# Talking-heads attention and an MLP on one core: x loaded a unit ahead, stores two units behind, first keys from two queues, and the second mixing with 128-column weights on two row halves

## The chip, the core and the metric

One core of a Trainium2 chip runs the whole program. The metric is device time in microseconds (us), the median of the runs of one kernel. Engines are named as in the profile: PE is TensorE (PEld its weight loads, which overlap its matmuls), DVE VectorE, ACT ScalarE, POOL GpSimd, SP SyncE. SP, ACT and POOL also issue DMAs from their own queues, in the order of their programs.

## What is computed

```python
def attn(q, k, v, w_pre, w_post):                 # 4 batches, 12 heads, 448 rows, 64 wide
    scores = (1 / 8) * q @ k.transpose(0, 1, 3, 2)
    scores = einsum('bhij,hg->bgij', scores, w_pre)      # first mixing of the heads
    attn = softmax(scores)                               # over j
    attn = einsum('bhij,hg->bgij', attn, w_post)         # second mixing
    return attn @ v

x = attn(...).transpose(0, 2, 1, 3).reshape(1792, 768)
h = x @ w_in                                      # 768 x 2048
out = maximum(0.01 * h, h) @ w_out                # 2048 x 768
```

All inputs and the output are float32.

## The kernel before, in words

The work has two stages. The **attention stage** goes over 16 chunks: each of the four batches has its 448 query rows cut into chunks of 120, 120, 120 and 88 rows. A chunk takes three **units** (`s` = 0, 1, 2), and `at` = 3n + s counts the 48 units. Several chunks are in flight: unit (n, s) does

- `scores` for chunk n + 2, two head pairs: PE writes `pss`, ACT moves it to the tile `st` (line 198);
- `first` for the next unit's rows: the first mixing, PE, `psm`, from the tiles `r`; then `maxima` (DVE, line 231) and `power` (ACT, line 241, the exponentials `et`);
- `weights` for this unit: DVE makes `kp`, the second mixing's matrix divided by the row sums;
- `mix` in two parts (lines 259 to 298): the second mixing, PE, `psa`. The weights of these matmuls are columns of `et`, which is why `mix` also transposes; the moving side is `kp`. Part 0 takes key chunks 0 and 1 and ACT copies its result to `at` (line 308); part 1 takes key chunks 2 and 3 and DVE copies it. Key chunk 3 holds 64 keys. A matmul of `mix` works on 64 of the 128 rows (`b`) and 64 of the 128 output partitions (`z`), so four of them lie side by side in the array;
- `values` for chunk n - 1: PE, `psx` from `at` and `vt`, then from `half` and `vend`; DVE copies it to `xo` (line 333) and SP stores a chunk's `xo` to `x_dram` (line 340).

Between chunks the scores change their layout by DMA: `regroup` (line 207) reads `st` and writes the twelve tiles `r`, even ones from SP's queue, odd ones from POOL's (line 212). The table `REGROUP` says in which of the chunk's twelve slots (three units of four) the pairs of tiles are issued.

Beside this, the MLP's weights arrive in a packed form and are put together in the attention stage by `Narrow`: SP loads `craw` (line 96), ACT spreads it (lines 102 and 103), DVE assembles (108 to 115), POOL joins (119 and 120) and SP stores `w` to `w_dram` (line 123). A store is issued at the start of the unit after the join.

The last six units (`at` = 42 to 47) run through `end_period` (line 625). In them `x_work` brings in the attention's result for the **MLP stage**: `load_x` (line 357) issues four DMAs `xr<-x_dram` (line 362), and `prep_x` (line 366) makes seven operands of them, one for each `k`. An operand is a pair `xh` (ACT, line 386) and `xl` (DVE, line 387); for k = 2, 3, 4 and 6 POOL first takes a difference (lines 374, 377, 379, 381). `x_plan` says in which slot which load or operand is made. The tiles `xr` come from a pool of five; the difference of k = 2 has a tile of its own, `xt`.

The MLP stage (`hidden`, `project`) multiplies in three products of split operands and is one long run of matmuls on PE.

Before the first unit come the warm-up matmuls `idle`, the first queries and the first keys: SP issues twelve DMAs `kt<-in_k` in a row (line 156), then the queries of chunk 1 (line 167).

Every engine works through its instructions in the order in which this code issues them (`pin`); only the plain calls of the MLP stage are left to the scheduler.

Of the kernel before, what the change touches and what calls it, by code (L numbers as in the profile page):

```python
# [8 lines left out]
F32 = mybir.dt.float32  # L9
# [14 lines left out]
PIECE = 384  # L24
RUN = 2
QUAD = 2 * ROWS
REGROUP = (0, 1, 3, 5, 7, 9)


def chunks_of(S):  # L30
# [4 lines left out]
def kernel(  # L35
# [10 lines left out]
    nc = tc.nc  # L46
    B, P, NJ, H, D = v.shape
    S = k.shape[3]
# [7 lines left out]
    HALF = SLOTS // 2  # L56
    HP = P // 2
    HC = NC // 2
    XS = 8
    HALF_IN = HC * P  # L60
    scale = 1.0 / math.sqrt(D)
    assert NC == 2 * HC and NF % 2 == 0 and B % 2 == 0
# [65 lines left out]
    pool = pools(left, "left")  # L128
# [5 lines left out]
    pool = pools(psum, "left")  # L134
# [3 lines left out]
    pool = pools(right, "right")  # L138
    p_q = pool("q", 2)
    p_k = pool("k", 2 * NPAIR)  # L140
    pool = pools(top, "left")
# [3 lines left out]
    pin = tc.keep_in_program_order  # L145
# [3 lines left out]

    k_t, q_t, v_t, s_t, r_t, e_t, kp_t, at_t, xo_t = ({} for _ in range(9))  # L150

    def load_k(b, a):
        t = k_t[b, a] = p_k.tile([P, S], F32, tag="k", name="kt")
        for e in range(2):
            up = slice(D * e, D * (e + 1))
            pin(nc.sync.dma_start(t[up], k[b, up, 2 * a + e, :]))

    def width(n):
        return -(-chunks[n][2] // QUAD) * QUAD
# [99 lines left out]
    def mix(n, s, part):  # L259

        sg = chunks[n][3][s]
        if s == part == 0:
            at_t[n] = (
                p_at.tile([P, (NJ - 1) * H, CHUNK], F32, tag="at", name="at"),
                p_at.tile([P, NPAIR, CHUNK], F32, tag="half", name="half"),
            )  # L270
        at, half = at_t[n]
        es, kp, nu, R = e_t[n, s][0], kp_t[n, s], len(sg), ROWS // 2
        ps = ps_x.tile([P, 2, 512], F32, tag="x", name="psa")
        per = nu * ROWS
        outs, done = [], 0
        for c in ((0, 1), (2, NJ - 1))[part]:
            nh = H if c < NJ - 1 else NPAIR
            outs.append(ps[:, :, done:done + nh * per])
            out = outs[-1].rearrange("p b (h u w) -> p b h u w", h=nh, w=ROWS)
            done += nh * per  # L280
            for g, e in enumerate(es):
                for z in range(2):
                    for b in range(2):
                        up, to = slice(HP * b, HP * (b + 1)), slice(HP * z, HP * (z + 1))
                        keys, step = (c * P + HP * z, 1) if nh == H else (c * P, 2)
                        mm(
                            out[to, b, :, g // 2, R * (g % 2):R * (g % 2 + 1)], e[up, keys:keys + HP],
                            kp[up, g, (z if step == 2 else 0)::step], start=True, stop=True,
                        )
        cols = slice(QUAD * sg[0], QUAD * sg[0] + QUAD * nu)  # L290
        if part == 0:
            moves = [(at[:, :2 * H], ps[:, :, :done], nc.scalar.copy)]
        else:
            moves = [(at[:, 2 * H:], outs[0], nc.vector.tensor_copy), (half, outs[1], nc.vector.tensor_copy)]
        return [(
            copy, to[:, :, cols].rearrange("p h (u b w) -> p b h u w", b=2, w=ROWS),
            src.rearrange("p b (h u w) -> p b h u w", u=nu, w=ROWS),
        ) for to, src, copy in moves]
# [44 lines left out]
    pl = {}  # L343

    def open_x():
        pool = pools(mlp, "right")
        pl.update(xr=pool("xr", 5), xs=[pool("xs0", XS)])

    def open_mlp():
        pool = pools(mlp, "right")  # L350
# [13 lines left out]
    X_PARTS = 7  # L364

    def prep_x(p, c, k, add=nc.vector, hold=free):

        x = [[xr_t[p, c, h, e] for e in range(2)] for h in range(2)]
        if k == 2:
            xr_t[p, c] = pl["xr"].tile([P, S], F32, tag="xr", name="xt")
            hold(add.tensor_sub(xr_t[p, c], x[0][1], x[0][0]))
        t = xr_t.get((p, c))
        if k == 3:
            hold(add.tensor_sub(x[0][1], x[1][1], x[0][1]))
        if k == 4:
            hold(add.tensor_sub(t, x[1][1], t))
        if k == 6:  # L380
            hold(add.tensor_sub(x[1][0], x[1][0], t))
        name, raw = ((1, x[0][0]), (2, x[1][0]), (5, t), (7, x[0][1]), (6, t), (3, x[1][1]), (4, x[1][0]))[k]
        pool = pl["xs"][X_PARTS * c + k >= XS]
        hi = pool.tile([P, S], F32R, tag="xh", name="xh")
        lo = pool.tile([P, S], F32R, tag="xl", name="xl")
        hold(nc.scalar.copy(hi, raw))
        hold(nc.vector.tensor_sub(lo, raw, hi.bitcast(F32)))
        x_t[name, c] = hi, lo
# [132 lines left out]
    nc.scalar.activation(warm, warm, AF.Exp)  # L521
    load_q(0, nc.scalar, nc.sync)
    for a in range(NPAIR):
        load_k(0, a)
    load_q(1)
    for t in r_all:
        nc.vector.memset(t[:LOW], 0.0)
# [62 lines left out]
            piece.assemble()  # L590
            joining.append(piece)

    x_plan = {0: [-1], 9: [6, -2], 17: [13, -3]}
    x_plan.update({i + 3: [i] for i in range(6)})
    x_plan.update({i + 4: [i] for i in range(7, 13)})
    x_plan.update({i + 5: [i] for i in range(14, 19)})

    def x_work(n, t):
        for i in x_plan.get(t + SLOTS * (n - NCK + 2), ()):
# [25 lines left out]
    def end_period(n, s):  # L625

        nonlocal kept, pending
        at = 3 * n + s - 42
        if kept:
            keep_x(*kept)  # L630
            kept = None
        for piece in joining:
            piece.join()
        storing.extend(joining)
        joining.clear()
        if at == 0:
            right.close()
            open_x()
            store_x(n - 2)
        if at == 3:  # L640
            top.close()
            open_mlp()
            load_wi(0)
            store_x(n - 2)
        if at == 4:
            mixed.close()
            pool = pools(mlp, "right")
            pl.update(ws=pool("ws", 1), ps_h=pool("ps_h", 1, space=PSUM))
        early, late = ((2, 0), (2, 1), (2, 1), (1, 0), (0, 0), (0, 0))[at]
        if pending:  # L650
            keep_at(mix(*pending, 1))
            pending = None
        weights(n, s)
        dues = [first(*left_quads.pop(0)) for _ in range(early)]
        for due in dues:
            maxima(*due)
        for c in range(NJ):
            transfers(n, s, c)
            x_work(n, NJ * s + c)
        for due in dues:  # L660
            power(*due)
        keep_at(mix(n, s, 0))
        assemble()
        keep_x(*values(n - 1, s))
        keep_at(mix(n, s, 1))
        for _ in range(late):
            due = first(*left_quads.pop(0))
            maxima(*due)
            power(*due)
        if at == 4:  # L670
            prep_wi(0, 0, pin)
        if at == 5:
            prep_wi(0, 1, pin)

    pending = None
    for n in range(NCK):
        b = chunks[n][0]
        last = n == NCK - 1
        for s in range(3):
# [2 lines left out]
            nxt = (n, s + 1) if s < 2 else (n + 1, 0)  # L682
            to, pair = n + 2, 2 * s

            for piece in storing:
                piece.store()
            storing.clear()
            if at >= 42:
                end_period(n, s)
                continue  # L690
# [12 lines left out]
            weights(n, s)  # L703
            for piece in joining:
                piece.join()
            storing.extend(joining)
            joining.clear()
            if pending:
                keep_at(mix(*pending, 1))
# [25 lines left out]
    hidden(0, 0, 0)  # L735
    for s in range(3):
        keep_x(*values(NCK - 1, s))
        if s:
            prep_x(0, HC - 1, X_PARTS - 3 + s, nc.gpsimd, pin)
    store_x(NCK - 1)  # L740
    psum.close()
    left.close()
# [108 lines left out]
```

## Time and profile before

| | us |
|---|---|
| median of 3 runs | 905.76 (905.28 to 906.59) |
| profiled execution, its time | 906.61 |
| profiled execution, its span | 904.7 |
| PE busy | 815.0, 90% of the span |
| DVE, ACT, POOL busy | 591.4, 487.7, 170.9 |

The span runs from the program's first instruction to its last. Busy time is a mean over stages: the attention stage ends near 443 us, and what bounds it is not what bounds the MLP stage. The granted clock of PE stands beside each stretch in the table by stretch. A matmul's end is modelled, so the pace of a row of matmuls is read from their starts, or from the time that the whole row takes.

### The profile page before, as it was taken

The page shows a single profiled execution, that of the slowest core. Times are in us where ns is not written, and L with a number is a line of the kernel's source. Part 1 is how long each engine was busy: PE and PEld are TensorE (multiplying, and loading weights), DVE is VectorE, ACT ScalarE, POOL GpSimd, SP SyncE. Part 2 cuts the span into 40 slices and gives each one's busy share as a digit, 9 for nine tenths or more (in the row PEclk, how much of TensorE's full clock was granted, in tenths as well). Part 3 has the DMA queues.
Part 4 walks back from the last instruction along what each step waited for, and adds up shares of the span by engine and source line. Part 5 has one row for each costly group of instructions (what it writes and reads, how often), then busy time and mean ns, then how long its engine had stood idle before and what let it go on. Part 6 is the DMA issues. An engine that isn't in the chain of part 4 may idle for free.

```text
span 904.7 us, 25819 instructions
## 1 busy us (share of the span) xinstructions
PE 815.0 (90%) x10904; PEld 652.1 (72%) x10904; DVE 591.4 (65%) x1063; ACT 487.7 (54%) x952; POOL 170.9 (19%) x224
## 2 busy tenths in 40 slices
PE   7789887989987989846779999999999999999998
PEld 2356655656655656634669999998999999999997
DVE  5478674786865767636588777876956656663433
ACT  3578784876866777545344444545644333332432
POOL 3245342443543444422200000000000000000000
PEclk9699997999999999978999999999999999999999
DMA  6899877997899879462255444535634222221533
GB/s 170 249 250 254 238 217 208 251 248 232 233 256 239 239 194 276 149 187 59 63 177 149 150 156 123 152 102 171 195 114 140 96 70 70 88 70 35 166 107 111
DMA packets 96526, 150.59 MB, mean 166 GB/s; under 512 B 38760, under 2 KB 72076, under 8 KB 96412
## 3 DMA queue, kind: packets, MB, share of 16 engines
q1 hardware_dynamic: 86728, 126.19, 48.4%
q0 software_dynamic: 7296, 19.40, 7.8%
q10 hardware_dynamic: 2388, 3.37, 1.0%
q8 instruction: 85, 1.39, 0.7%
q14 instruction: 29, 0.24, 0.1%
HBM read 85.73 MB, written 23.59 MB: 121 GB/s over the span
## 4 chain that ended last, share of the span: by engine, by line
PE 74%; DMA 7%; issue 6%; ACT 6%; DVE 5%; SPq 1%; POOL 1%; ACTq 0%; DVEq 0%; POOLq 0%
PE pso L148 25%; PE psh L148 22%; PE psx L148 8%; PE psm L148 6%; PE pss L148 6%; PE psa L148 6%; ACT st L198 3%; ACT et L241 2%; DMA xr<-x_dram 1%; SPq L212 1%; DMA r<-st 1%; DVE stat L231 1%; DMA qt<-in_q 1%; PE idle L148 1%; DVE at L308 1%
## 5 line engine op out<-in xcount | busy, mean ns | idle before, releaser
L148 PEld LDWEIGHTS psa<-kp,et 64*64 64x64 f32 x5888 | 109.9, 139 | 97.0 <-issue 45.2
L148 PE MATMUL psa<-kp,et 64*64 64x60 f32 (+1 forms) x5888 | 114.4, 222 | 50.0 <-issue 20.7
L148 PE MATMUL pso<-gh,wl 128*128 128x448 f32 x384 | 140.9, 367 | 1.2 <-DVE wl L395 1.2
L148 PE MATMUL pso<-gh,wh 128*128 128x448 f32 x384 | 140.5, 366 | 0.0
L148 PE MATMUL pso<-gl,wh 128*128 128x448 f32 x384 | 140.4, 366 | 0.0
L198 ACT ACTIVATE st<-pss 120x896 f32<-120x896 f32 (+1 forms) x84 | 77.5, 923 | 85.1 <-PE pss L148 80.5
L241 ACT ACTIVATE et<-psm,stat 128x448 f32<-128x448 f32 x184 | 115.8, 646 | 13.2 <-DVE stat L231 8.4
L394 ACT CAST wh<-wo 128x768 fp32r<-128x768 f32 x64 | 53.5, 836 | 128.9 <-PE pso L148 115.4
L395 DVE TENSOR_TENSOR wl<-wo,wh 128x768 fp32r<-128x768 f32 x64 | 61.2, 956 | 87.1 <-ACT wh L394 86.7
L231 DVE TENSOR_REDUCE stat<-psm 128x2 f32<-128x896 f32 x92 | 99.6, 1085 | 25.4 <-PE psm L148 25.3
L148 PE MATMUL pss<-kt,qt 64*64 64x448 f32 (+2 forms) x768 | 97.8, 554 | 15.3 <-issue 7.4
L148 PE MATMUL psm<-r,kpre 64*64 64x448 f32 x736 | 98.0, 596 | 3.8 <-DMA r<-st 2.4
L148 PEld LDWEIGHTS pso<-gh,wl 128*128 128x128 f32 x384 | 72.1, 188 | 8.8 <-DVE wl L395 2.3
L148 PE MATMUL psx<-at,vt 128*64 128x120 f32 (+1 forms) x1152 | 71.5, 274 | 7.7 <-issue 3.0
L148 PEld LDWEIGHTS pso<-gh,wh 128*128 128x128 f32 x384 | 72.1, 188 | 6.0
L148 PEld LDWEIGHTS pso<-gl,wh 128*128 128x128 f32 x384 | 72.1, 188 | 5.9
L148 PEld LDWEIGHTS pss<-kt,qt 64*64 64x64 f32 (+2 forms) x768 | 31.2, 131 | 61.0 <-issue 35.1
L119 POOL TENSOR_TENSOR w<-w,z 128x384 f32<-128x384 f32 x48 | 47.9, 997 | 133.8 <-ACT at L308 88.8
L148 PEld LDWEIGHTS psx<-at,vt 128*64 128x64 f32 x1152 | 59.9, 141 | 17.3 <-issue 7.6
L212 POOL DMA_DIRECT2D r<-st x90 | 55.4, 617 | 89.9 <-ACT st L198 55.0
L333 DVE COPY xo<-psx 128x240 f32<-128x240 f32 (+1 forms) x48 | 27.2, 566 | 36.3 <-PE psx L148 36.0
L308 ACT COPY at<-psa 128x960 f32<-128x960 f32 x44 | 43.4, 986 | 13.2 <-PE psa L148 13.0
(103 smaller groups left out, 1441.8 us busy)
## 6 DMA issues: line engine op xcount, KB each, us to landing
craw<-in_w_moe SPq DMA_DIRECT2D x64, 384.0 KB
wo<-w_dram SPq DMA_DIRECT2D x64, 384.0 KB
r<-st SPq DMA_DIRECT2D x92, 210.0 KB
r<-st POOLq DMA_DIRECT2D x90, 210.0 KB, 6.3
wi<-w_dram SPq DMA_DIRECT2D x34, 384.0 KB
w_dram<-w SPq DMA_DIRECT2D x64, 192.0 KB
kt<-in_k SPq DMA_DIRECT2D x48, 112.0 KB
xr<-x_dram SPq DMA_DIRECT2D x24, 224.0 KB
```

The lines of the kernel that those rows point to most:

```text
L119: pin(self.joiner.tensor_mul(w, w, self.exp))
L148: pin(nc.tensor.matmul(*args, **kw))
L198: pin(nc.scalar.activation(to, ps, AF.Copy, scale=scale))
L212: pin((queues or (nc.sync, nc.gpsimd))[g % 2].dma_start(t[LOW:LOW + RH], s_t[n][g:m:m // ROWS]))
L231: pin(nc.vector.tensor_reduce(e_t[n, s][1][:, 0, 2 * u:2 * u + 2], ps[:, :, :S], axis=AX.X, op=ALU.max, negate=True))
L241: pin(nc.scalar.activation(e, ps[:, y, :S], AF.Exp, bias=st[:, 0, g:g + 1], accum_out=st[:, 1, g:g + 1]))
L308: pin(copy(to, src))
L333: pin(nc.vector.tensor_copy(xo_t[n][:, RUN * s:RUN * (s + 1), :m].rearrange("p a (x g) -> p a g x", x=ROWS), ps[:, :RUN, :m].rearrange("p ...
L394: hold(nc.scalar.copy(hi, raw))
L395: hold(nc.vector.tensor_sub(lo, raw, hi.bitcast(F32)))
```

## The change

Six edits, given here with their diffs.

The second mixing's matmuls for key chunks 0 to 2 have 128 weight columns instead of 64, on 64 rows; those for key chunk 3 stay.

```diff
             for g, e in enumerate(es):
-                for z in range(2):
+                for z in range(H // nh):
                     for b in range(2):
                         up, to = slice(HP * b, HP * (b + 1)), slice(HP * z, HP * (z + 1))
-                        keys, step = (c * P + HP * z, 1) if nh == H else (c * P, 2)
+                        if nh == H:
+                            to = slice(0, P)
                         mm(
-                            out[to, b, :, g // 2, R * (g % 2):R * (g % 2 + 1)], e[up, keys:keys + HP],
-                            kp[up, g, (z if step == 2 else 0)::step], start=True, stop=True,
+                            out[to, b, :, g // 2, R * (g % 2):R * (g % 2 + 1)],
+                            e[up, c * P:c * P + to.stop - to.start], kp[up, g, z::H // nh], start=True, stop=True,
                         )
```

The first keys are issued alternately by SP and ACT, and `regroup` moves by a slot:

```diff
-REGROUP = (0, 1, 3, 5, 7, 9)
+REGROUP = (1, 2, 4, 6, 8, 10)
...
-    def load_k(b, a):
+    def load_k(b, a, queue=nc.sync):
...
     for a in range(NPAIR):
-        load_k(0, a)
+        load_k(0, a, (nc.sync, nc.scalar)[a % 2])
```

The stores of `w` wait one unit more:

```diff
-            for piece in storing:
-                piece.store()
-            storing.clear()
+            while storing and storing[0][0] < at - (at < 43):
+                storing.pop(0)[1].store()
...
-            storing.extend(joining)
+            storing.extend((at, piece) for piece in joining)
```

The loads of x and the making of its operands are put in other slots, four at a time and ahead; the pool `xr` has eight tiles, the difference of k = 2 is written over the tile that k = 0 has read, and operands 3 to 6 of the last third are made between the last `values`:

```diff
-    x_plan = {0: [-1], 9: [6, -2], 17: [13, -3]}
...
+    x_plan = {0: [-1, -2], 4: [0, 1, 2], 8: [3, 4, 5], 12: [6, 7, 8, -3], 16: [9, 10, 11, 12], 20: [13, 14, 15, 16]}
...
-        pl.update(xr=pool("xr", 5), xs=[pool("xs0", XS)])
+        pl.update(xr=pool("xr", 8), xs=[pool("xs0", XS)])
...
         if k == 2:
-            xr_t[p, c] = pl["xr"].tile([P, S], F32, tag="xr", name="xt")
+            xr_t[p, c] = x[0][0]
             hold(add.tensor_sub(xr_t[p, c], x[0][1], x[0][0]))
...
     for s in range(3):
         keep_x(*values(NCK - 1, s))
-        if s:
-            prep_x(0, HC - 1, X_PARTS - 3 + s, nc.gpsimd, pin)
+        for k in ((3,), (4,), (5, 6))[s]:
+            prep_x(0, HC - 1, k, nc.gpsimd, pin)
```

(`XS`, which only divides the operands between two pools, goes from 8 to 6.)

What this does to the order on the engines is seen best at three places. The first is PE in one full unit of the attention stage. A matmul of float32 appears in the trace as two instructions, so the counts there are twice these. Before:

```order
L148 MATMUL psm<-r_126,kpre 64x448 x2
L148 MATMUL psm<-r_127,kpre 64x448 x2
L148 MATMUL pss<-kt,qt 64x448 x2
L148 MATMUL pss<-kt,qt 56x448 x2
L148 MATMUL psa<-kp,et 64x12x5 x16
L148 MATMUL psa<-kp,et 64x6x5 x16
L148 MATMUL psm<-r_128,kpre 64x448 x2
L148 MATMUL psm<-r_129,kpre 64x448 x2
L148 MATMUL pss<-kt,qt 64x448 x2
L148 MATMUL pss<-kt,qt 56x448 x2
L148 MATMUL psa<-kp,et 64x12x5 x32
```

The same unit on PE, now:

```order
L148 MATMUL psm<-r_126,kpre 64x448 x2
L148 MATMUL psm<-r_127,kpre 64x448 x2
L148 MATMUL pss<-kt,qt 64x448 x2
L148 MATMUL pss<-kt,qt 56x448 x2
L148 MATMUL psa<-kp,et 128x12x5 x8
L148 MATMUL psa<-kp,et 64x6x5 x16
L148 MATMUL psm<-r_128,kpre 64x448 x2
L148 MATMUL psm<-r_129,kpre 64x448 x2
L148 MATMUL pss<-kt,qt 64x448 x2
L148 MATMUL pss<-kt,qt 56x448 x2
L148 MATMUL psa<-kp,et 128x12x5 x16
```

Nothing moves; 48 of the unit's 64 second-mixing matmuls become 24 with twice the columns.

The second is ACT at the end of the attention stage, from the last `at` copy of unit 41 to that of unit 43. Before:

```order
L308 COPY at<-psa 128x2x24x2x10
L241 ACTIVATE et,stat<-psm,stat 128x448 x2
L386 CAST xh<-xr 128x448
L241 ACTIVATE et,stat<-psm,stat 128x448 x4
L308 COPY at<-psa 128x2x24x2x10
L386 CAST xh<-xr 128x448
L386 CAST xh<-xt 128x448
L386 CAST xh<-xr 128x448
L386 CAST xh<-xt 128x448
L241 ACTIVATE et,stat<-psm,stat 128x448 x4
L308 COPY at<-psa 128x2x24x2x10
```

ACT over the same units, now:

```order
L309 COPY at<-psa 128x2x24x2x10
L241 ACTIVATE et,stat<-psm,stat 128x448 x6
L309 COPY at<-psa 128x2x24x2x10
L387 CAST xh<-xr 128x448 x3
L241 ACTIVATE et,stat<-psm,stat 128x448 x4
L309 COPY at<-psa 128x2x24x2x10
```

Unit 42 has no operand of x any more, and unit 43 has three instead of four, of which the last one (k = 2) is a difference.

The third is SP's queue in units 42 and 43. Before:

```order
L123 DMA w_dram_75<-w 128x384
L340 DMA x_dram_79<-xo 768x1x120
L212 DMA r_124<-st 120x1x448
L362 DMA xr<-x_dram_76 128x448 x2
L362 DMA xr<-x_dram_77 128x448 x2
L212 DMA r_126<-st 120x1x448
L212 DMA r_128<-st 120x1x448
```

SP's queue from the same `x_dram` store on, now:

```order
L341 DMA x_dram_79<-xo 768x1x120
L363 DMA xr<-x_dram_76 128x448 x2
L363 DMA xr<-x_dram_77 128x448 x2
L363 DMA xr<-x_dram_76 128x448 x2
L363 DMA xr<-x_dram_77 128x448 x2
L212 DMA r_124<-st 120x1x448
L212 DMA r_126<-st 120x1x448
L123 DMA w_dram_75<-w 128x384 x2
L212 DMA r_128<-st 120x1x448
```

Eight loads of x stand in a row, and the `r` tile that stood ahead of the first of them now stands behind the last.

## Rows read from the trace of the kernel before

**Rows 1.** Table by stretch: busy time and instructions by engine, PE's clock, DMA share, GB/s.

```profile
61.00:377.00 316.00, 279.98 (x6931) 189.48 (x6928) 219.24 (x436) 230.87 (x495) 131.03 (x163) 0.98 0.85 234
377.00:443.00 66.00, 40.54 (x1040) 30.98 (x1036) 35.77 (x67) 28.45 (x68) 19.98 (x19) 0.84 0.36 103
...
468.00:901.00 433.00, 430.34 (x2105) 394.59 (x2104) 282.64 (x465) 185.13 (x304) 0.00 (x0) 1.00 0.38 118
```

**Rows 2.** Timeline of PE in one unit: start, us, what.

```profile
70.21 0.98 PE L148 MATMUL psm<-r,kpre 64*64 64x448 f32 x8
...
71.76 1.08 PE L148 MATMUL psa<-kp,et 64*64 64x60 f32 x64
72.66 0.96 PE L148 MATMUL psm<-r,kpre 64*64 64x448 f32 x8
...
74.20 1.11 PE L148 MATMUL psa<-kp,et 64*64 64x60 f32 x64
75.41 1.45 PE L148 MATMUL psx<-at,vt 128*64 128x120 f32 x24
76.80 0.70 PE L148 MATMUL psx<-half,vend 128*128 128x120 f32 x4
77.43 0.98 PE L148 MATMUL psm<-r,kpre 64*64 64x448 f32 x8
```

**Rows 3.** Timeline of the weight loads in that unit.

```profile
74.11 1.06 PEld L148 LDWEIGHTS psa<-kp,et 64*64 64x64 f32 x64 [0.52 <-PE psm L148]
...
76.79 0.52 PEld L148 LDWEIGHTS psx<-half,vend 128*128 128x128 f32 x4 [0.16 <-issue]
```

**Rows 4.** Weight loads from 61 to 377 us by shape: count, busy us, mean ns, idle.

```profile
L148 PEld LDWEIGHTS psa<-kp,et 64*64 64x64 f32 x4672 | 86.0, 135 | 62.3 <-issue 37.3 <-PE psm L148 13.5 <-PE pss L148 8.3
...
L148 PEld LDWEIGHTS psx<-half,vend 128*128 128x128 f32 x152 | 20.6, 197 | 6.0 <-issue 4.5 <-DMA kt<-in_k 0.3 <-DMA vt<-in_v 0.2
```

**Rows 5.** Timeline of PE: a run of 30-column second-mixing matmuls.

```profile
208.27 0.60 PE L148 MATMUL psa<-kp,et 64*64 64x30 f32 x28 [0.66 <-issue]
```

**Rows 6.** Matmuls of the whole program by shape.

```profile
L148 PE MATMUL psa<-kp,et 64*64 64x60 f32 x4416 | 91.4, 223 | 47.1 <-ACT at L308 17.8 <-issue 17.7 <-DVE kp L253 6.3
```

**Rows 7.** Timeline of PE: second mixing followed by values, unit 42.

```profile
382.21 1.16 PE L148 MATMUL psa<-kp,et 64*64 64x60 f32 x64 [0.38 <-DVE kp L253]
383.30 1.45 PE L148 MATMUL psx<-at,vt 128*64 128x120 f32 x24
```

**Rows 8.** Timeline of ACT in the unit of rows 2.

```profile
74.44 0.92 ACT L198 ACTIVATE st<-pss 100x896 f32<-100x896 f32 x1 [0.29 <-PE pss L148]
```

**Rows 9.** Waits of PE from 40 to 400 us: total, times, longest.

```profile
PE psa L148 <- issue: 20.7, 15, 4.2
...
PE pss L148 <- issue: 7.4, 3, 3.0
PE psx L148 <- issue: 3.0, 4, 1.5
```

**Rows 10.** The page: PE's instructions, and the queue that brings them (packets, MB).

```profile
PE 815.0 (90%) x10904; PEld 652.1 (72%) x10904; DVE 591.4 (65%) x1063; ACT 487.7 (54%) x952; POOL 170.9 (19%) x224
...
q8 instruction: 85, 1.39, 0.7%
```

**Rows 11.** Table by stretch, from the end of one long "issue" wait to the next.

```profile
272.07:279.82 7.75, 3.54 (x127) 2.79 (x127) 3.25 (x6) 3.93 (x8) 2.45 (x3) 1.00 0.94 211
```

**Rows 12.** Waits of PE from 377 to 443 us.

```profile
PE psa L148 <- ACT at L308: 17.0, 4, 7.8
```

**Rows 13.** Waits of ACT from 377 to 443 us.

```profile
ACT xh L386 <- POOL xt L379: 14.8, 3, 7.0
ACT xh L386 <- DMA xr<-x_dram: 9.9, 1, 9.9
```

**Rows 14.** Timeline of PE at the start: warm-up, first scores.

```profile
1.60 6.15 PE L148 MATMUL idle<-vend 128*128 128x448 f32 x8 [1.60 <-POOL wt L530]
...
7.68 4.73 PE L148 MATMUL pss<-kt,qt 64*64 64x448 f32 x48
```

More of the change, by code (lines that the diff above doesn't have):

```diff
@@ L58 @@
     HC = NC // 2
-    XS = 8
+    XS = 6
     HALF_IN = HC * P
@@ L155, in load_k @@
             up = slice(D * e, D * (e + 1))
-            pin(nc.sync.dma_start(t[up], k[b, up, 2 * a + e, :]))
+            pin(queue.dma_start(t[up], k[b, up, 2 * a + e, :]))
     def width(n):
@@ L591, in assemble @@
             joining.append(piece)
-    x_plan = {0: [-1], 9: [6, -2], 17: [13, -3]}
-    x_plan.update({i + 3: [i] for i in range(6)})
-    x_plan.update({i + 4: [i] for i in range(7, 13)})
-    x_plan.update({i + 5: [i] for i in range(14, 19)})
+    x_plan = {0: [-1, -2], 4: [0, 1, 2], 8: [3, 4, 5], 12: [6, 7, 8, -3], 16: [9, 10, 11, 12], 20: [13, 14, 15, 16]}
     def x_work(n, t):
@@ L633, in end_period @@
             piece.join()
-        storing.extend(joining)
+        storing.extend((at + 42, piece) for piece in joining)
         joining.clear()
@@ L705 @@
                 piece.join()
-            storing.extend(joining)
+            storing.extend((at, piece) for piece in joining)
             joining.clear()
```

## The prediction

> **What bounds the kernel now.** I read the table by stretch first [rows 1]. The MLP stage is PE without a gap (430 of 433 us at full clock); no edit takes or adds a matmul there, so its 433 us stand. What can change lies before 443 us: the main part of the attention stage (61 to 377 us, 38 units, PE busy 280 of 316) and its end (377 to 443, PE busy 41 of 66, clock 0.84).
>
> Next the timeline of one unit without a hole [rows 2]. From 70.21 to 77.43 us every group of matmuls starts where the one before lets it: mixing and scores 1.55 us twice, second mixing part 1 0.90, part 0 1.21, values 1.39 and 0.63; together 7.22. PE sets the pace of such a unit, so a matmul made dearer there costs its full time. 38 units of 7.22 are 274 us against 316, so some 42 us of the main part are waiting. The table of waits names most of it: "issue", 20.7 + 7.4 + 3.0 = 31.1 us in 22 waits [rows 9]. What is behind it is seen between the ends of two such waits: 127 matmuls and 127 weight loads, 256 instructions with two lost records [rows 11]. PE's program came as 85 packets of 1.39 MB for 21,808 instructions [rows 10], that is 64 bytes each and 256 to a packet. So PE's code arrives in blocks of 256, and PE stands where the next block is late.
>
> **What sets the pace of the second mixing.** Four tiles of 64 x 64 work side by side, so 64 instructions are 16 rounds. The weight loads took 1.06 us for them, the last alone 0.135: (1.06 - 0.135) / 15 = 0.062 us a round; from the starts in rows 2 the first 16 rounds took 0.90, 0.056 each. I take 0.058 [rows 2 to 4]. A run of 28 matmuls of 30 columns, 7 rounds, took 0.60 us with 0.22 for its last, so 0.063 [rows 5]: half the moving columns go no faster. The round is set by loading 64 weight columns, not by streaming.
>
> **The change: the loads.** For key chunks 0 to 2, 4416 instructions in rounds of four [rows 6], 1104 rounds, become 2208 in rounds of two, again 1104 rounds, each now with 128 columns to load. The only 128-column loads of float32 in this stage are those of the last matmuls of `values`, full height: four took 0.52 us, the last 0.197, so (0.52 - 0.197) / 3 = 0.108 us [rows 3, 4]. A load of half the height stands in no row. Its bounds are 0.058 (two half-width loads side by side do this now) and 0.22 (the two halves wait for each other); I take 0.108, since the column count is the same as in the nearest row and all four tiles load at once today. That is 1104 x (0.108 - 0.058) = **+55 us**, between 0 and +177.
>
> By the Trainium skill, "TensorE: Matmul & The Clock Gate", section "LDWEIGHTS (loading the stationary operand)", a load takes its columns over 1.2 GHz whatever the number of rows, 53 ns for 64 and 107 ns for 128, which would make it +59 us. The rows agree as to the columns; as to half the height, no row here shows it.
>
> **The change: other costs of the same edit.** The array's division now changes between the scores (64 x 64) and this mixing (64 x 128), twice around part 1 and once more ahead of part 0. The four full-width matmuls of `values` take 0.63 us from start to start although four loads need 0.43: 0.20 for the two changes around them [rows 2]. Second mixing to `values` took 1.09 us with 0.93 of rounds, 0.16 for one [rows 7]. I take 0.10: 48 units x 3 x 0.10 = **+14 us** (0 to +23). Against it: in the unit shown, `values` waited for ACT's move of `st`, which ended at 75.36 [rows 8] while the mixing's rounds ended near 75.2; a longer part 0 uses this up, about 0.12 us in 38 units, **-5**.
>
> The counts fall too. Of a unit's 188 matmuls (376 instructions) 140 are left (280). A block of 256 instructions lasted 7.22 x 256 / 376 = 4.9 us of work; with a unit of some 8.6 us it lasts 7.9. A late block now has 3 us more, and the longest "issue" wait was 4.2 [rows 9]. I leave 2 us of the 31: **-29**. The main part's clock of 0.98 [rows 1] is 6 us of lost pace, which goes with the long waits as PE then does not fall idle: **-4**.
>
> **The change: x ahead.** At the end PE waited 17.0 us for ACT's copy of `at` [rows 12], and ACT stood in front of that copy on operands of x: 9.9 us for the load of x and 14.8 for POOL's difference [rows 13]. Unit 42 has no operand now, so the first goes whole; its PE wait was 7.8. In unit 44 (k = 3, 4, 5) and unit 45 the differences need nothing that DVE makes in the same unit, so ACT no longer waits there. In unit 43 (k = 2, over the tile that k = 0 reads) POOL must wait for DVE's `xl` of k = 0, which stands behind two row maxima, so about half of that wait stays, and the exponentials behind it wait with it. I take 13 of the 17 us, and 5 of the some 10 that a clock of 0.84 over 66 us costs: **-18** (-27 to 0). What is late next: eight loads in SP's queue ahead of the `r` tile for chunk 15. The load that ACT awaited for 9.9 us was one of four, so eight may need twice that; the tile is wanted only at the end of unit 43, and I put 0 to +5. Two more operands lie between the last `values`: **+1**.
>
> **Edits that I cost at nothing.** First keys from two queues: the first scores start at 7.68 us, as the warm-up matmuls end (1.60 + 6.15), and six pairs take 4.73 us without a hole [rows 14]; PE's own work covers the loads. If the keys were the limit there, it would be worth 1 us. `regroup` a slot later and the stores of `w` two units behind take waits off SP and POOL; PE's waits name neither, and its cover is the lead of several slots between an `r` tile's load and its use. If that lead goes, a chunk start waits: 14 chunks x 0 to 1 us.
>
> **The sum.** 55 + 14 - 5 - 29 - 4 - 18 + 1 = +14 us on the profiled execution's 906.6, which is 0.85 above the median of the runs: about **920 us**.
>
> **Rivals.** *The half-height load is as fast as two half-width ones.* Then a round stays at 0.058 us, the first term is 0, the unit is near 7.5 us, a block lasts 6.9 us and some 24 us of "issue" go: 14 - 5 - 24 - 4 - 18 + 1 = -36, **870 us**. It decides from a round under 0.095 us on (14 / 1104 below 0.108). For it: four half-width loads do run at once. Against it: a 128-column load took 0.108. Chance 0.10.
>
> *The longer mixing swallows every wait.* The 42 us of waiting in the main part go whole (9 more than my 33), as every other engine gains 1.3 us a unit, and the end gives its full 27: 14 - 9 - 9 = -4, **902 us**. For it: DMA was busy 0.85 of the main part, and slower units ease it. Against it: some of the 42 us are waits for copies that follow the mixing itself. Chance 0.15.
>
> *Load and matmul of one half take turns*, or the halves do. Then a round costs 0.108 + 0.05 or more: **over 970 us**, up to 1040. By the Trainium skill, the same page, Part 3, "The mechanism", a weight load overlaps a running matmul only where the row groups differ, which would give this; the trace speaks against it. Its row: matmuls of 120 columns on two tiles took 1.45 us for 12 rounds [rows 2], so streaming alone takes about 0.11, and four full-height loads and matmuls in turn would need over 0.85 us where they took 0.63. Chance 0.05.
>
> **How the numbers follow.** My case 0.70, within it 905 to 938 us (round 0.100 to 0.115, change of division 0.05 to 0.15, end -10 to -24). The range leaves out the first and the third rival and a little of each end: **890 to 940**. A measurement of this kernel tells about 0.2% from no change. Slower by more: my case but for 0.05 of it, and the third rival, 0.70. Within 0.2%: 0.06, from my case's low end and the second rival's high one. Faster: the first rival and most of the second, 0.24.
>
> **What would show it.** The new profile should have 64 x 128 weight loads at one round per 0.11 us; part 0 near 1.8 us and part 1 near 1.4; "issue" waits of PE under 5 us; no wait of ACT for the load of x; the stretch from the last full unit to the first MLP matmul shorter by about 9 us, mixing included; the main part longer by 15 to 22. A round under 0.095 us or a main part no longer than before would prove me wrong.

## The result and the profile after

The changed kernel takes **916.09 us** (median of 4 runs, 914.62 to 921.57) against 906.17 (905.28 to 912.54) for the kernel before: a ratio of 1.0105, 95% interval 1.006 to 1.015. It is slower, by about 9.5 us; 920 was forecast, with a range of 890 to 940. A time is the median of all runs, while a ratio leaves out the runs that stood clearly above the others of their kernel; f4 below was profiled only in such a run (908.8 us, with 6.1 us of "issue"), so its stretches are not compared. The profiled execution spans 914.9 us where that of before spanned 904.7.

Two lines of the page of the changed kernel, busy time and instructions by engine, and the queue that brings PE's program, answer to [rows 10]:

```profile
PE 881.1 (96%) x8696; PEld 702.4 (77%) x8696; DVE 593.8 (65%) x1063; ACT 491.9 (54%) x952; POOL 168.6 (18%) x224
...
q8 instruction: 68, 1.11, 0.5%
```

PE has 2208 matmuls fewer and is busy for 66 us more. The table by stretch of the changed kernel (columns as in [rows 1]), cut near the first `values`, which is that of unit 3 (`at` = 3), and near that of unit 41:

```profile
59.00:385.50 326.50, 324.99 (x5176) 222.18 (x5174) 220.64 (x435) 234.20 (x494) 130.01 (x164) 1.00 0.84 226
385.50:452.00 66.50, 54.33 (x731) 43.41 (x731) 34.96 (x63) 27.77 (x65) 17.25 (x17) 0.77 0.36 104
```

In the main part PE is now busy for 325 of 326.5 us, where it was busy for 280 of 316; its clock is 1.00 there and 0.77 in the end (0.84 before). Counted between the starts of `values` of units 3, 41 and 47, the main part went from 316.2 to 326.8 us (+10.6) and the end from 62.4 to 63.4 (+1.0); what lies ahead took 2.3 us less, what follows 0.9 more. Together +10.2, the whole difference of the spans. (The expectations below count units from the first `values` on: their units 0, 38 and 44 are these.)

The timeline of PE in one unit of the changed kernel, beside [rows 2]:

```profile
76.21 1.45 PE L148 MATMUL psx<-at,vt 128*64 128x120 f32 x24
77.59 0.70 PE L148 MATMUL psx<-half,vend 128*128 128x120 f32 x4
78.22 0.98 PE L148 MATMUL psm<-r,kpre 64*64 64x448 f32 x8
79.03 0.93 PE L148 MATMUL pss<-kt,qt 64*64 64x448 f32 x8
79.89 1.70 PE L148 MATMUL psa<-kp,et 64*128 64x60 f32 x48
81.42 0.96 PE L148 MATMUL psm<-r,kpre 64*64 64x448 f32 x8
82.20 0.93 PE L148 MATMUL pss<-kt,qt 64*64 64x448 f32 x8
83.06 2.00 PE L148 MATMUL psa<-kp,et 64*128 64x60 f32 x32
84.99 1.25 PE L148 MATMUL psx<-at,vt 128*64 128x120 f32 x20
```

From `values` to `values` it is 8.78 us where it was 7.22. Part 1 takes 1.53 (0.90 before), part 0 1.93 (1.21), and the scores ahead of each 0.86 (0.75). The weight loads of part 0 in the same unit:

```profile
83.06 1.86 PEld L148 LDWEIGHTS psa<-kp,et 64*128 64x128 f32 x32 [0.71 <-PE psm L148]
```

With 0.19 us for the last, 32 loads on two row halves are 16 rounds at (1.86 - 0.19) / 15 = 0.111 us. The table of waits of PE from 40 to 400 us, beside [rows 9]; its columns are total, times and longest:

```profile
PE psa L148 <- DVE half L309: 1.3, 3, 0.5
PE psa L148 <- DVE kp L253: 0.8, 2, 0.4
PE psa L148 <- ACT at L309: 0.4, 1, 0.4
PE pss L148 <- ACT st L198: 0.2, 1, 0.2
```

Of the 31.1 us of "issue" nothing is left. Units of the main part with full chunks alone take 8.78 us, but for one of 9.22; the kernel before scattered between 7.2 and 14.1 there. Last, the waits of PE and of ACT in the end (385.5 to 452 us), beside [rows 12, 13]:

```profile
PE psa L148 <- DVE kp L253: 6.7, 5, 2.6
PE psa L148 <- ACT at L309: 4.3, 2, 3.9
```

```profile
ACT xh L387 <- POOL xr L375: 13.4, 2, 6.8
ACT et L241 <- DVE stat L231: 10.5, 3, 5.8
ACT xh L387 <- POOL xr L380: 5.6, 1, 5.6
```

ACT no longer waits for a load of x, and PE's wait for `at` fell from 17.0 to 4.3 us.

### The profile page after: what moved, and what is told of

It is laid out like the page before. It is cut to its first block, busy times and chain, and to the rows that moved or that the text cites. A ratio compares the mean times of both kernels' runs of the same rounds, so it can differ in the third digit from the quotient of the medians.

```text
span 914.9 us, 21387 instructions
## 1 busy us (share of the span) xinstructions
PE 881.1 (96%) x8696; PEld 702.4 (77%) x8696; DVE 593.8 (65%) x1063; ACT 491.9 (54%) x952; POOL 168.6 (18%) x224
## 4 chain that ended last, share of the span: by engine, by line
PE 89%; DMA 5%; DVE 3%; issue 1%; ACT 1%; SPq 1%; ACTq 0%; POOL 0%; DVEq 0%; POOLq 0%
PE psh L148 22%; PE pso L148 22%; PE psa L148 18%; PE psx L148 10%; PE psm L148 8%; PE pss L148 8%; DMA xr<-x_dram 2%; DMA wo<-w_dram 1%; DMA qt<-in_q 1%; DMA craw<-in_w_moe 1%; PE idle L148 1%; ACTq L212 0%; DMA out_t<-o 0%; ACT et L241 0%; DVE wl L396 0%
## 5 line engine op out<-in xcount | busy, mean ns | idle before, releaser
L148 PEld LDWEIGHTS psa<-kp,et 64*128 64x128 f32 (+1 forms) x3680 | 161.9, 170 | 79.8 <-issue 36.8
L148 PE MATMUL psa<-kp,et 64*128 64x60 f32 (+1 forms) x3680 | 176.7, 258 | 12.3 <-DVE kp L253 6.7
L241 ACT ACTIVATE et<-psm,stat 128x448 f32<-128x448 f32 x184 | 114.9, 634 | 18.1 <-DVE stat L231 12.7
L396 DVE TENSOR_TENSOR wl<-wo,wh 128x768 fp32r<-128x768 f32 x64 | 61.1, 957 | 86.0 <-ACT wh L395 85.6
L148 PE MATMUL pss<-kt,qt 64*64 64x448 f32 (+2 forms) x768 | 95.9, 554 | 5.7 <-DVE st L202 3.4
L148 PE MATMUL psm<-r,kpre 64*64 64x448 f32 x736 | 94.4, 580 | 2.2 <-ACT et L241 2.2
L212 POOL DMA_DIRECT2D r<-st x90 | 53.3, 595 | 18.3 <-DMA r<-st 8.4
L108 DVE TENSOR_SCALAR top<-z 128x384 uint32<-128x384 uint32 x64 | 24.2, 378 | 38.5 <-ACT z L102 37.9
```

Of the source, the lines that this page charges most:

```text
L108: pin(nc.vector.tensor_scalar(top, z.bitcast(U32), 3, 0x7FFFFFF8, op0=ALU.logical_shift_left, op1=ALU.bitwise_and))
L148: pin(nc.tensor.matmul(*args, **kw))
L212: pin((queues or (nc.sync, nc.gpsimd))[g % 2].dma_start(t[LOW:LOW + RH], s_t[n][g:m:m // ROWS]))
L241: pin(nc.scalar.activation(e, ps[:, y, :S], AF.Exp, bias=st[:, 0, g:g + 1], accum_out=st[:, 1, g:g + 1]))
```

## The experiments

Two theories stood. **Mine**: the wider loads make every unit longer, the longer unit hides the late blocks of PE's program, and x ahead shortens the end. **The rivals**: the waits depend on something other than the unit's length; or one of the edits costed at nothing has a price. The kernels were timed apart from the pair above, those named e on one chip and those named f and g on another, each beside the kernel before, which took 907.5 to 910.9 us there; so ratios to that are compared. All times of main part and end go from `values` to `values` as above.

### One part alone

**e1_mix_only**: the kernel before with the mixing's edit and nothing else.

```diff
-                for z in range(2):
+                for z in range(H // nh):
...
-                        keys, step = (c * P + HP * z, 1) if nh == H else (c * P, 2)
+                        if nh == H:
+                            to = slice(0, P)
...
```

> The kernel before with the second mixing's edit alone; loads of x, stores, first keys and regroup as before. Theory (the mixing adds about 1.5 us to each unit and its smaller code frees the main part of the waits for code): main part at 8.8 us a unit, 38 units 327 us, 'issue' waits of PE under 3 us; the end of the stage keeps its waits for x and pays the mixing too, so about 8 us more than in the changed kernel: 920 to 927 us. Rival (the other five edits did nothing for the time): 914 to 918 us, as the changed kernel.

Measured: 930.9 us (921.69 to 934.18), ratio 1.0187 [1.0111, 1.0264]. The main part is 326.3 us at 8.78 a unit without "issue", as in the changed kernel. The end grew from 62.4 to 77.8 us, which put the time above both forecasts. The table by stretch:

```profile
61.00:387.00 326.00, 324.77 (x5176) 222.33 (x5174) 220.24 (x436) 234.42 (x495) 131.74 (x164) 1.00 0.82 226
387.00:465.00 78.00, 62.80 (x712) 49.41 (x710) 34.40 (x65) 27.54 (x65) 17.54 (x18) 0.63 0.30 86
```

One line of PE's waits in its end:

```profile
PE psa L148 <- ACT at L309: 8.0, 3, 6.8
```

So the mixing alone makes the main part what it is in the changed kernel. In the end six units of 1.56 us would be 9 at full clock. It grew by 15, at a clock of 0.63 (0.84 in [rows 1]), although PE waited 9 us less for `at` than before; what lowered the clock was not varied by itself.

**e2_rest_only**: the changed kernel with the old mixing.

```diff
-                for z in range(H // nh):
+                for z in range(2):
...
```

> The changed kernel with the second mixing as before: the five other edits alone. Theory: the 'issue' waits are back (25 us or more from 40 to 400 us), main part 312 to 318 us for 38 units; the end is 6 to 10 us shorter than before since ACT no longer waits for the load of x: 893 to 900 us. Rival (the five edits also took the waits for code away, by moving DMAs): main part below 300 us, 'issue' under 10 us, 880 to 888 us. Second rival (the end's gain is lost to a low clock whatever the mixing): 903 to 907 us.

Measured: 904.46 us (898.49 to 919.14), ratio 0.9892 [0.9822, 0.9962]. The end is 50.8 us (-11.6), the main part 324.1 (+7.9 on before), and the waits are back; three lines of PE's waits from 60 to 384 us:

```profile
PE psa L148 <- issue: 24.9, 16, 4.0
PE psx L148 <- issue: 7.6, 4, 3.6
PE pss L148 <- issue: 1.9, 2, 1.0
```

The waits on blocks go with the narrow mixing. But a main part 8 us longer than that of before, without the mixing's edit, had no place in the prediction. The next two took it apart.

**f1_x_only**: the kernel before with x ahead (plan, pools, k = 2's tile, the tail) and nothing else.

```diff
-    x_plan = {0: [-1], 9: [6, -2], 17: [13, -3]}
...
+    x_plan = {0: [-1, -2], 4: [0, 1, 2], 8: [3, 4, 5], 12: [6, 7, 8, -3], 16: [9, 10, 11, 12], 20: [13, 14, 15, 16]}
...
```

> The kernel before with the edits of x alone (loads and operands ahead, pool of eight); second mixing, regroup, stores and first keys as before. Theory (the gain at the end is x's): from the last full unit's values to the last unit's values 49 to 54 us instead of 62.4, ACT never waits for the load of x; main part 312 to 322 us for 38 units with 25 us or more of 'issue'. Ratio 0.983 to 0.993. Rival (it takes regroup and the stores moved as well): 57 to 63 us at the end, ratio 0.995 to 1.003.

Measured: 897.76 us (889.77 to 903.83), ratio 0.9853 [0.9755, 0.9951]. The end is 52.7 us (-9.7), its clock 0.85. The main part is 320.8 us (+4.6), with 31.4 us of "issue".

**f2_queues_only**: the kernel before with the first keys from two queues, the regrouping a slot later and the later stores.

```diff
-REGROUP = (0, 1, 3, 5, 7, 9)
+REGROUP = (1, 2, 4, 6, 8, 10)
...
-        load_k(0, a)
+        load_k(0, a, (nc.sync, nc.scalar)[a % 2])
...
-        storing.extend(joining)
+        storing.extend((at + 42, piece) for piece in joining)
...
```

> The kernel before with first keys from two queues, regroup a slot later and stores two units behind, and nothing else. Theory (these edits move waits of SP and POOL that PE does not see): end 61 to 64 us, main part 312 to 322 us, ratio 0.996 to 1.005. Rival (they are what made the main part 324 us in the run without the mixing's edit): main part 322 to 330 us, 'issue' over 33 us, ratio 1.005 to 1.015.

Measured: 919.91 us (914.01 to 930.39), ratio 1.0134 [1.0052, 1.0216], main part 329.3 us. The edits that I costed at nothing cost about 12 us where the mixing is narrow. Two more kernels split them; the first keys were not tried alone.

**g3_regroup_only**: only the first two lines of that diff.

> The kernel before with the regrouping of each chunk's results started one step later, and nothing else. It asks which of the edits of the queues made that experiment 1.3% slower. Theory 1 (the regrouping): ratio 1.005 to 1.015, units from 0 to 38 of 322 to 330 us against 316, waits put down to issue of 33 to 40 us. Theory 2 (the later stores): ratio 0.996 to 1.004, units of 314 to 320 us. Theory 3 (both shift which block of instructions is late, and neither has a price of its own): a ratio between, with other stretches of half clock.

Measured: 914.37 us (910.27 to 927.02), ratio 1.0110 [1.0068, 1.0152]; main part 322.1 us. "Issue" did not grow as the first theory had it; from 60 to 384 us it is 22.6 + 2.6 + 2.0 + 1.3 = 28.5 us, against 28.1 in the kernel before. Another wait grew. Waits of ACT from 60 to 384 us in this kernel:

```profile
ACT st L198 <- DMA w_dram<-w: 4.7, 2, 2.5
ACT st L198 <- DMA r<-st: 3.3, 1, 3.3
ACT st L198 <- DMA craw<-in_w_moe: 2.8, 1, 2.8
ACT st L198 <- DMA kt<-in_k: 2.7, 1, 2.7
```

and in the kernel before:

```profile
ACT st L198 <- DMA vend<-in_v: 2.9, 1, 2.9
ACT st L198 <- DMA kt<-in_k: 1.7, 1, 1.7
```

ACT's moves of the scores waited 13.5 us for DMAs instead of 4.6. One of them on ACT's timeline, and the same place on PE's:

```profile
286.31 0.92 ACT L198 ACTIVATE st<-pss 120x896 f32<-120x896 f32 x1 [3.31 <-DMA r<-st]
```

```profile
287.28 0.98 PE L148 MATMUL pss<-kt,qt 64*64 64x448 f32 x8 [2.06 <-ACT st L198]
```

A `st` tile is written again two chunks later (its pool holds two), and must first have been read by the regrouping. A slot later for the last pair takes one of the three slots between that read's issue and the next write. At this place ACT then stands, `pss` is not emptied, and PE stands; PE's waits of this kind rose from 0.9 to 4.5 us in all. The other DMA names in the list are taken for the same wait from the code alone; the 3.3 us are shown. That this is what costs the 1.1% is not shown, as the table behind the next kernel says.

**g4_stores_only**: only the last two lines of that diff, with the loop that issues them. (The "regrouped results" of the expectation are the tiles `w`.)

> The kernel before with the stores of the regrouped results moved two units behind, and nothing else. Theory 1 (the regrouping is what costs): ratio 0.996 to 1.004, units from 0 to 38 of 314 to 320 us. Theory 2 (the stores cost, since they then stand on their queue beside other loads): ratio 1.005 to 1.015, units of 322 to 330 us, and waits put down to issue of 33 to 40 us. Theory 3 (neither has a price of its own): a ratio between, with other stretches of half clock.

Measured: 910.26 us (904.58 to 917.43), ratio 1.0020 [0.9981, 1.0060], main part 314.4 us. Within its interval the stores cost nothing. All kernels with the narrow mixing and nothing added to their units, each by its one profiled execution; the waits are PE's and ACT's in the main part, in us:

| | regrouping | main part, us | PE, "issue" | PE, `pss` for ACT's `st` | ACT, `st` for DMAs |
|---|---|---|---|---|---|
| g4_stores_only | as before | 314.4 | 25.0 | 0.2 | 6.1 |
| before | as before | 316.2 | 28.1 | 0.9 | 4.6 |
| f1_x_only | as before | 320.8 | 31.4 | 0.3 | 2.2 |
| g3_regroup_only | later | 322.1 | 28.5 | 4.5 | 13.5 |
| e2_rest_only | later | 324.1 | 34.4 | 0.2 | 6.1 |
| f3_rest_x_later (below) | later | 326.7 | 33.2 | 2.0 | 12.1 |
| f2_queues_only | later | 329.3 | 33.4 | 2.6 | 8.5 |

The four with the later regrouping have the longest main parts, and g3's ratio is clear of 1 while g4's isn't: of the queue edits it is the regrouping that costs. How is open. "Issue" and the waits for `st` both tend to grow with it, but `pss` accounts for 3.6 of g3's 5.9 us and for nothing in e2. Before and f1 differ only behind the main part and are 4.6 us apart, so a few us of one execution mean little.

**g2_mix_and_x**: the changed kernel with the old regrouping, stores and first keys.

> The whole change without its edits of the queues: 128-column weights in both parts, x loaded ahead as in the change, but the regroup, the stores and the first keys as before. Theory (with the longer mixing the order of these queues costs nothing, as the prediction had it): units from 0 to 38 at 8.78 us each, 326 to 328 us in all, no waits put down to issue, and an end as in the changed kernel, 61 to 65 us; a ratio of 1.005 to 1.013 to the kernel before. Rival (the edits of the queues cost with either mixing the 1.3% that they cost with the narrow one): units of 318 us or less and a ratio of 0.990 to 1.000.

Measured: 915.62 us (912.26 to 926.30), ratio 1.0074 [1.0033, 1.0116]; main part 326.3 us at 8.78 a unit. PE's waits from 60 to 387 us are this one line:

```profile
PE psa L148 <- DVE half L309: 1.2, 3, 0.4
```

With the wide mixing the queue edits cost about the 0.3% between 1.0074 and 1.0105, which the intervals don't tell from nothing. That the longer unit covers them is argued: in the changed kernel ACT's moves of `st` still wait 7.9 us for DMAs in the main part, and PE waits 0.2 us for them.

### Is it the length of a block?

**e3_pad**: the kernel before with two matmuls of no use after each unit's `values`, which make a unit about as long as in the changed kernel, but with more instructions and not fewer.

```diff
+        for _ in range(2):
+            mm(both[:, 1, :S], flat[:, :P], flat[:, :S], start=True, stop=True)
...
```

> The kernel before with two more matmuls of 128 x 448 behind each unit's values, into PSUM that nothing reads: 1.5 us of PE more a unit, as the changed mixing costs, but 384 instructions a unit instead of 280. Theory (a block of 256 instructions must arrive in the time PE takes for the one ahead): a block lasts 5.8 us against 7.9, so 8 to 18 us of 'issue' are left from 40 to 400 us, and the main part's unit is 9.0 to 9.3 us on average; 923 to 935 us. Rival (any slower unit swallows the waits): 'issue' under 3 us and 8.75 us a unit, 915 to 922 us.

Measured: 945.88 us (944.04 to 949.67), ratio 1.0373 [1.0313, 1.0433]. (The absolute time expected was too low: 48 units of 1.5 us are 72, and about half of that was won back.) A unit without waits takes 8.73 us. The waits on blocks, from 60 to 410 us:

```profile
PE psx L148 <- issue: 9.3, 9, 2.2
```

All nine stand in `values`; the longest is 2.2 us. A longer unit alone thus took two thirds of the waits; the last third, 9.3 us, stays where the changed kernel, in units of the same length, has none.

**f4_part0_wide** and **g1_part0_x** put a fourth point between: 128 columns in part 0 alone, and only up to unit 41, with a later plan for x (e4 below). f4 has the change's queue edits, g1 has not.

```diff
-                for z in range(2):
+                wide = nh == H and part == 0 and 3 * n + s < 42
+                for z in range(1 if wide else 2):
...
```

> As f3, and the second mixing with 128 columns in part 0 alone and in units 0 to 41 alone: 312 instructions a unit. Theory (a unit costs its rounds and changes of division, and a late block costs what it exceeds the time of the block ahead): 8.1 to 8.2 us a full unit, a block of 6.7 us, 3 to 9 us of 'issue'; main part 308 to 315 us, end as f3; ratio 0.970 to 0.983. Rival (code waits do not depend on the instructions in a unit): 25 us of 'issue' and a main part over 330 us, ratio above 1.

> The kernel before with x loaded ahead (a later plan than the change's) and with the 128-column weights in part 0 of the mixing alone, in the units before 42; part 1, the last units' mixing, the regroup, the stores and the first keys stay as they were. It has 312 TensorE instructions in a unit: 256 + 56. Theory (code arrives in blocks of 256 instructions, and a unit that is long enough for its instructions hides their arrival; the end wants narrow mixing and early x): a unit without waits takes 7.22 + 0.82 = 8.0 to 8.1 us, waits put down to issue come to 4 to 12 us in the units from 0 to 38 where the kernel before has 31, these units take 304 to 315 us (316 before, 327 with the whole change) and the end 48 to 53 us; the time stands at 0.970 to 0.985 of the kernel before. Rival (the waits have little to do with a unit's length): issue 25 us or more, units 335 us or more, ratio 1.000 or above.

Measured: f4 891.68 us (888.39 to 908.76), ratio 0.9844 [0.9782, 0.9907], just above the range expected. g1 **891.36 us** (887.86 to 894.01), ratio **0.9793** [0.9741, 0.9845]: faster than both kernels. Its end is 47.3 us and its waits on blocks are fewer than expected. Its table by stretch, and PE's "issue" waits from 60 to 385 us:

```profile
62.73:376.25 313.52, 307.05 (x5762) 212.18 (x5760) 217.52 (x436) 233.62 (x495) 131.79 (x164) 0.98 0.85 234
...
376.25:423.50 47.25, 34.34 (x978) 26.26 (x976) 32.66 (x61) 26.95 (x63) 14.83 (x15) 0.94 0.47 143
```

```profile
PE psa L148 <- issue: 1.7, 1, 1.7
```

The four kernels in one table; a block's length is the unit without waits times 256 over its instructions (matmuls and loads), and the last column is all the time that PE was not busy in the main part:

| | unit, us | instructions | a block, us | "issue" in the main part, us | PE idle, us |
|---|---|---|---|---|---|
| before | 7.22 | 376 | 4.9 | 28.1 | 36.1 |
| e3_pad | 8.73 | 384 | 5.8 | 9.3 | 18.3 |
| g1_part0_x | 8.05 | 312 | 6.6 | 1.7 | 6.5 |
| after | 8.78 | 280 | 8.0 | 0 | 1.5 |

The waits fall with the length of a block, not of a unit: g1's unit is shorter than e3's and waits less. The steps are clear of the scatter: the seven kernels with blocks of 4.9 us have 25.0 to 34.4 us of "issue", the four with the wide mixing in both parts none. Nor do less busy DMA engines explain it: their share was 0.76 in e3 and 0.85 in g1. What makes a block late in the first place wasn't tried.

### The end

**e4_x_later**: the changed kernel with its operands of x some slots later, so that fewer stand ahead of `at` and the exponentials on ACT.

```diff
-    x_plan = {0: [-1, -2], 4: [0, 1, 2], 8: [3, 4, 5], 12: [6, 7, 8, -3], 16: [9, 10, 11, 12], 20: [13, 14, 15, 16]}
+    x_plan = {0: [-1, -2], 4: [0, 1, 5], 8: [2, 3], 12: [4, 6, 7, 8, -3], 16: [9, 10, 12], 20: [11, 13, 14, 15]}
...
-        for k in ((3,), (4,), (5, 6))[s]:
+        for k in ((2, 3), (4,), (5, 6))[s]:
```

> The changed kernel with the operands of x in other units: a difference is taken only in a unit after the one that made the xl which it must wait for (k = 0, 1, 5 in unit 43; 2, 3 in unit 44; 4, 6 and the next third's 0, 1 in unit 45; and so on). Theory: the 3.9 us wait of PE at 403 us is gone, the clock keeps its full level there, and the stretch from the last full unit to the MLP is 6 to 11 us shorter: 905 to 911 us. Rival (the clock falls at the end anyway, as PE has too little work there): 2 to 4 us, 912 to 915 us.

Measured: 913.31 us (908.76 to 916.55), ratio 1.0045 [1.0003, 1.0087]; main part 326.3 us, end 58.5 against 63.4. The 3.9 us wait is gone (0.9 us are left of PE's waits for `at` in the end), but the clock there is 0.81, not full, and the end gained 4.9 us, between theory and rival.

**f3_rest_x_later**: the same plan with the old mixing.

> The five edits without the mixing's, and the differences of x a unit after the xl that they wait for. Theory: the end loses the wait for POOL in unit 43 and most of its time at half clock, 45 to 49 us instead of 50.8; main part as without it, 312 to 325 us; ratio 0.978 to 0.990. Rival (with the narrow mixing the wait is hidden): 50 to 52 us, ratio 0.986 to 0.993.

Measured: 902.94 us (894.73 to 914.49), ratio 0.9934 [0.9887, 0.9980]; end 48.9 us at a clock of 0.91, as the theory had it; the main part, 326.7, is above it, and with it the time. The plan takes 5 us off the end with the wide mixing and 2 with the narrow one (50.8 in e2).

## Why the prediction came out

**The sum was right by 4 us, by terms that were not.** Forecast were +14 on the span; +10.2 came. By place, my terms put about +17 on the main part, -9 on the end and +6 on the other four units; measured were +10.6, +1.0 and -1.4. Three misses of 6, 10 and 7 us offset each other to 4, so the nearness of 920 and 916 is in part luck. Two of the signs named beforehand didn't come: the main part was to grow by 15 to 22 us, and the stretch behind it to shrink by 9.

**The price of the mixing: right, a little low.** A round takes 0.111 us where I took 0.108 from the full-height loads, so half the height is no cheaper and the two row halves do load side by side. A full unit has 24 such rounds: 24 x (0.111 - 0.058) = 1.27 us of the 1.56. My "-5 hidden" came out. In the end, where ACT moves no scores, part 0 took 1.09 us before [rows 7] and takes as long in the changed kernel as in its main part, 1.93:

```profile
391.07 2.00 PE L148 MATMUL psa<-kp,et 64*128 64x60 f32 x32 [0.38 <-DVE kp L253]
393.00 1.45 PE L148 MATMUL psx<-at,vt 128*64 128x120 f32 x24
```

So it grew by 0.84 us there and by 0.72 in the main part, where the 0.12 us of waiting for `st` went. The term that was too small is the change of division. The scores ahead of the two parts began here in the kernel before (the mixing's starts are in [rows 2]):

```profile
71.01 0.93 PE L148 MATMUL pss<-kt,qt 64*64 64x448 f32 x8
73.45 0.94 PE L148 MATMUL pss<-kt,qt 64*64 64x448 f32 x8
```

From there to the mixing it was 0.75 us and is 0.86 now, 0.11 more each time, and part 1 took 0.21 more than its eight wide rounds account for: 0.43 us for the three changes, where I took 0.30. In the 38 units of the main part the mixing came to some 58 us, against 50 by my terms. The first and the third rival (a round under 0.095, or over 0.158) fall.

By the Trainium skill, "TensorE: Matmul & The Clock Gate", section "LDWEIGHTS (loading the stationary operand)", a load takes its columns over 1.2 GHz whatever the number of rows, which makes an estimate of 107 ns for 128 columns. The trace agrees, with 0.111 us for half the rows. By the Trainium skill, the same page, Part 3, "The mechanism", a load overlaps a running matmul only where the row groups differ. The trace doesn't bear that out here: with load and matmul of one half in turn a round would take 0.158 us or more, as the third rival had it, and it takes 0.111, the load alone.

**The waits: the mechanism right, its size too small.** I let 2 of 31 us of "issue" stand and left other waits as they were; in the changed kernel all "issue" is gone, and PE is idle for 1.5 us of the main part. The 42 us of waiting that I read from 38 units of 7.22 were too few as well, since the units with a short chunk are shorter. Were every unit of before as short in proportion as the full one, its main part without waits would be 326.8 x 7.22 / 8.78 = 269 us (an estimate); so some 47 us went where my terms had 33, and the mixing put 58 in their place. That is the second rival's mechanism for the main part: the mixing swallows every wait. It failed in the end, where it counted on the full 27 us and the end grew by 1.0.

**The end: the wait went, the gain did not.** PE's wait for `at` fell by 12.7 us; I had said 13. The part of k = 2 that I left standing is the 3.9 that is still there: ACT's `xh` waits 6.7 us for POOL's difference (up to 403.07 us), which waits for DVE's `xl`. The step that failed is the clock, which was to give back 5 us and fell instead: 0.77 over 66.5 us is 66.5 x 2 x 0.23 = 31 us at half clock, against 66 x 2 x 0.16 = 21 before [rows 1], and half of that time is lost, so it cost 4.7 us more than before. With -12.7 for the wait and 6 x 1.56 = +9.4 for the mixing at full clock that makes +1.4 (an estimate), where +1.0 was measured. Part of the loss is the mixing's own, since I costed it at full clock throughout. At half clock it takes nearly twice as long, as part 0 of unit 44 shows on PE's timeline of the changed kernel, at a granted clock of 0.50:

```profile
415.35 3.67 PE L148 MATMUL psa<-kp,et 64*128 64x60 f32 x32
```

It took 2.00 above. The two parts of the change pull in opposite directions in the one stretch where PE isn't at full pace: x ahead alone is worth 10 to 12 us of end (f1, e2), the mixing alone costs 15 there (e1), together they gave +1.0.

**Ahead of the first `values`: a price that did not show.** I put the mixing's cost on every unit, some 4 us on the three ahead of the first `values`. But four kernels with the wide mixing reach the first `values` at 58.7 to 61.1 us, eight with the narrow one at 57.8 to 62.3. Before and after, the stretch ahead of it reads (columns as in [rows 1]):

```profile
34.00:61.00 27.00, 21.69 (x568) 12.38 (x561) 17.70 (x32) 21.82 (x47) 9.64 (x13) 0.92 0.89 254
```

```profile
34.00:61.00 27.00, 27.00 (x414) 17.16 (x410) 19.58 (x35) 24.04 (x52) 10.51 (x15) 0.97 0.90 266
```

PE was idle for 5.3 us there in the kernel before, and the mixing's time seems to have gone into that; this is argued from the idle time alone.

**The edits costed at nothing: right here, wrong as a rule.** In the changed kernel they cost nothing that can be told from noise (g2). In the narrow one the regrouping costs 1.1% (g3). The prediction named a loss of lead as the danger and put it at the tile `r`; at the one place followed here it is the write of `st`, and where the rest of the 1.1% arises stays open. First keys from two queues: the first scores begin as the warm-up matmuls end in either kernel, and they end at 14.4 to 14.5 us in both.

**What the change was worth by parts**, as ratios to the kernel before: mixing 1.019, x ahead 0.985, queues 1.013, all three 1.0105. The product of the three is 1.017. That the whole stays below it would fit a price of the regrouping that the wide mixing hides, but the intervals are too wide to show it.

## What to carry to other kernels

A wait that an edit hides by making the work longer is no gain until it is set against the work that was added: here some 47 us of waiting left, and 58 us of longer mixing came. Take the cheapest part of such an edit that brings the waits down (part 0 alone gave nearly all of it), and look at its price by itself in stretches where PE's clock is down. Before costing a moved transfer at nothing, count the slots to the next write of the tile that it reads too, not only to the next read of the tile that it fills, and time it alone.

## What the runs showed of the hardware beyond this

- PE's program comes in blocks of 256 instructions (85 packets for 21,808 before, 68 for 17,392 after), and in these four kernels what late ones cost falls steeply with the time that a block lasts: 28.1, 9.3, 1.7 and 0 us at 4.9, 5.8, 6.6 and 8.0 us a block, with a DMA share of 0.84 to 0.85 in three of them and of 0.76 in e3.
- The same weights took 0.058 us a round as four loads of 64 columns and 0.111 us as two loads of 128. The time went by the columns of one load, and four loads ran beside each other as well as two. Half as many instructions thus took twice as long on the engine; what they saved is code.
- PE's granted clock was 1.00 in the main part of the changed kernel, where PE was idle for 1.5 us, and 0.63 over 78 us in the end of e1, where it waited up to 6.8 us at a time: between the two levels of 2.4 and 1.2 GHz. In the kernel before, waits of up to 7.8 us left 0.84 in the end, so the longest wait alone doesn't set it.
